# A new order for the first part of an attention and two-layer MoE kernel, and later places for the last attention pairs

## The chip, the cores and the metric

The kernel runs on one core of one Trainium2 chip. The metric is the device time of one launch in microseconds (us). The kernel before takes 853.68 us, the median of 3 runs (851.36 to 854.92).

## The reference

Three stages follow one another: an attention with two branches, a feed-forward layer with a gate (MoE 1), and one with a leaky relu (MoE 2).

```python
# attention: 4 batches, 8 heads, 576 positions, 64 features
q_d, k_d, v_d = [x.reshape(B, H, S // 4, 4, D).mean(axis=3) for x in (q, k, v)]
out_d = sm_attn(q_d, k_d, v_d)               # softmax over 144 pooled keys
out_up = np.repeat(out_d, 4, axis=2)
mask = np.abs(pos[:, None] - pos[None, :]) < 4
out_local = softmax(np.where(mask, scale * q @ k.T, -1e9)) @ v
x = out_up + out_local                       # to (2304 tokens, 512)
# MoE 1, then MoE 2, each 512 -> 2048 -> 512
h = x @ w_in;  g = h / (1 + np.exp(-1.702 * h));  x = g @ w_out
h = x @ w_in;  g = np.maximum(0.01 * h, h);       x = g @ w_out
```

The layers' weights arrive as float64 and are taken apart into a high and a low float32r part in the kernel. A product in MoE 1 is the sum of three matmuls: high by high, high by low, low by high.

## The kernel before

**Attention.** 16 jobs, one for each batch and pair of heads: job n is batch n // 4, pair n % 4. A job computes the scores in the band and those over the pooled keys, the two softmaxes, transposes the probabilities (`pt`, `pdt`, or by way of DRAM for late jobs: `td`, `pT`, `tdd`, `pdT`), multiplies with the values (`av` L684 and L700, `avd` L632 and L700) and adds the two results (`x`, L734).

**MoE 1.** 80 units: 5 blocks of tokens (512, 512, 512, 384, 384) by 16 chunks of the hidden dimension. A unit is its first layer (`l1_part`, L860: 12 matmuls into `h`), its gate (L879 on ScalarE, L880 on VectorE, a high copy L159, a low part L886) and its second layer (`l2`, L901: 12 matmuls into the four `acc` banks). The input of a block is split into `xh` (L159, ScalarE) and `xl` (L843) for each of its four feature chunks.

**Weights.** A chunk is loaded (L168), its sign and exponent taken by ScalarE (L187), its low word shifted (L188) and joined (L192) by VectorE, the high part copied (L159) and the low part subtracted (L211). The loaded words lie in one of three staging buffers, so the load of a chunk waits until the joining step of the chunk three loads earlier has read its buffer. MoE 2 follows from 491 us on and is not touched.

**What sets the order.** The kernel is under a manual schedule: each engine works through its instructions in the order in which the program issues them. The first part is a list of tokens, `ORDER` (L52 to L82): jobs 0 to 7, the weights of MoE 1, and its first 14 units, one token for each step. `w.n` loads half chunk n, `wF wL wB wH wO` are the five steps named above; `S` are the scores in the band, `E` their exponentials, `Rc` the reciprocal of the sums (L519, L520), `Mu` the division (L482), `T`/`U` the transposes and `C`/`D` the copies of them, `Va`/`Vb` the pooling of values (L440), `Kd`/`Qd` that of keys and queries (L427), `Vd` and `Y` the products with the values, `X` the sum of both branches, `xh`/`xl` the two parts of a feature chunk, `h0`/`h1` the first matmuls of units 0 and 1 by feature chunk, `L.n` the first layer of unit n, `Gt Gd Gh Gl` its gate, `M.n` its second layer. `.n` is the job, half chunk or unit. `z3.14` are 14 matmuls on a tile of zeros into bank `acc3`, whose result nobody reads (L1225). A token ends in `@V` or `@G` where it runs on VectorE or GpSimd rather than on its usual engine.

Block 0 of MoE 1 needs the first 512 tokens of all four pairs of batch 0, so `L.2`, the first unit issued in one piece, needs `xh.3` and `xl.3`, which need pair 3's `Y` products, which need its transposes, which need `Mu.3`.

From unit 14 on a loop goes over the units. After the gate of unit u come the steps listed under turn 2u, then (here, around unit 33) the second layer of the unit two before, then the steps under turn 2u+1. The later jobs 8 to 15 put their groups of steps there: group i of job n at turn `TURN + PERIOD*(n-JOBS) + i`, which is 24 + 6(n-8) + i.

Of the kernel before, what the change touches and what calls it, by code (L numbers as in the profile page):

```python
# [27 lines left out]
def attn_moe_kernel(ctx: ExitStack, tc, qT_d, kT_d, vh_d, vg_d, w1a, w2a, w1b, w2b, outT):  # L28
    nc = tc.nc
    B, NP = qT_d.shape[:2]  # L30
    DM, NT = outT.shape
# [15 lines left out]
    V, G = nc.vector, nc.gpsimd  # L47
# [5 lines left out]
        w.2 wF.2 wL.2 k.0 Kd.0 wB.2 wH.2 q.0 Qd.0 z3.14 S0.0 M0.0 S1.0 M1.0 va.4 Va0.4 Va1.4 w.0 wF.0 Sd.0 Mxd.0 Exd.0  # L53
        wO.2 wL.0 N0.0 E0.0 N1.0 Rcd.0 Mud.0 wB.0 wH.0 wO.0 k.1 q.1 z3.16 S0.1 Qd.1 Kd.1 M0.1 w.3 wF.3 wL.3 q.2 Sd.1
        Mxd.1 E1.0 Rc.0 Exd.1 vb.4 Vb0.4 wB.3 wH.3 wO.3 Vb1.4 Mu.0 Rcd.1 Mud.1 N0.1 E0.1 T0.0 C0.0 T1.0 C1.0 q.4 k.4
        z3.1 S.4 A1.4 k.2 va.1 w.1 wF.1 S1.1 M1.1 A0.4 Qd.2 Kd.2 Mx.4 Sb.4 z3.4 S0.2 M0.2 w.5 vb.7 wF.5 Qd.4 Sd.2 Mxd.2
        Exd.2 U0.0 D0.0 wL.5 N1.1 Kd.4 T0.1 k.3 z3.6 Sd.4 Rcd.2 Mud.2 wL.1 E1.1 Mxd.4 Exd.4 T1.1 C1.1 q.3 N0.2 E0.2 wB.5
        wH.5 wB.1 vb.2 Rc.1 Mu.1 Rcd.4 Mud.4 q.5 vb.0 k.5 z3.5 S.5 Qd.5 A1.5 Qd.3 A0.5 Kd.3 z3.6 U1.1 D1.1 S1.2 T0.2
        Kd.5 w.7 M1.2 wH.1 C0.1 wO.5 Vb0.7 U1.0 D1.0 wO.1 Mx.5 Sb.5 N1.2 Sd.3 S0.3 M0.3 Mxd.3 T1.4 wF.7 wL.7 va.0 T1.2
        w.4 wF.4 wL.4 w.6 wF.6 N0.3 wB.7 wB.4 E1.2 Rc.2 Mu.2 Ex.5 Exd.3 Rcd.3 Mud.3 C0.2 T0.4 C0.4 z3.4 S1.3 Vd.0 M1.3  # L60
        vh.0 Y0.0 k.6 va.6 va.5 vb.1 vh.4 C1.2 Od.0 X0.0 U0.1 D0.1 E0.3 wH.7 wO.7 C1.4 Ex.4 Y1.0 vh.1 va.2 vh.2 w.12
        vb.3 Vd.1 Od.1 w.9 X1.0 xh.0 wL.6 xl.0 N1.3 E1.3 Sm.5 wB.6 Sm.4 Rc.4 Mu.4 Rc.5 Sd.5 Mxd.5 T0.3 C0.3 Vd.4 Od.4
# [5 lines left out]
        Vb1.5 L.6 wF.15 Va0.6 wL.15 wB.19 Gt.3 wO.14@V wB.15 T0.5 T1.5 C0.5 w.10 wF.10 wL.10 wH.19 wO.19 M.0 M.1 C1.5
        Vd.5 Gd.3 Gh.3 Gl.3 wB.10 wH.10 wO.10 Va1.6 Sd.6 Mxd.6 M.2 L.4 Od.5@V va.7 w.16 Gt.6 Gd.6 wF.16 wL.16 Exd.6 w.11
        wF.11 Rcd.6 Gh.6 wL.11 wB.11 wH.11 wB.16 wH.15 Gl.6@V wO.15 S.6 A0.6 A1.6 Mx.6 Mud.6 Sb.6 wO.11@V Gt.4 Gd.4  # L70
        wH.16 wO.16@V w.22 Gh.4 Gl.4@V wF.22 wL.22 vh.5 w.13 wF.13 wL.13 vb.6 w.20 wF.20 wL.20 M.3 U1.5 D1.5 U0.5 D0.5
        wB.13 wH.13 wO.13 L.5 Gt.5 wB.20 wH.20 Gd.5 Gh.5 Gl.5 Ex.6 wB.22 wH.22 wO.22 L.7 q.7 Qd.7 k.7 Kd.7 S.7 A1.7
        wO.20 Sm.6 Gt.7 Gd.7 M.4 w.18 wF.18 wL.18 wB.18 Gh.7 Gl.7@V wH.18 wO.18 Rc.6 A0.7 Mx.7 Sb.7 w.17 wF.17 wL.17 L.8
        Gt.8 Gd.8 M.5 M.6 Y0.5 t.22 w.24 X0.5 Gh.8 Gl.8@V Vb0.6 w.26 wF.26 wL.26 wB.26 Y1.5 L.9 Gt.9 wH.26 T1.6 C1.6
        w.28 wB.17 Gd.9 Gh.9 L.10 X1.5 Sd.7 Ex.7 wO.26 Mu.6@V wH.17 Gl.9@V wO.17 M.7 M.8 Sm.7 Gt.10 Gd.10 Rc.7 wF.24
        wL.24 wF.28 wL.28 wB.24 w.21 wF.21 wL.21 Mxd.7 wB.21 wB.28 wH.24 Gh.10 Gl.10@V Vb1.6 U0.6 D0.6 Exd.7 Rcd.7 Va0.7
        wH.28 L.11 Gt.11 Gd.11 T0.6 C0.6 U1.6 D1.6 Gh.11 wO.24 Mu.7@V Mud.7 wO.28@V M.9 w.23 wF.23 wL.23 wH.21 Vd.6 Od.6
        vh.6 Y1.6 w.25 wF.25 w.27 X1.6 Va1.7 Gl.11@V wB.23 wO.21@V Vb1.7 wL.25 wB.25 wF.27 wL.27 wH.23@V wO.23 L.12
        Gt.12 Gd.12 T0.7 C0.7 T1.7 L.13 t.25 wH.25 wO.25@V C1.7 w.29 w.31 Y0.6 X0.6 U0.7 D0.7 Gh.12 wF.29 wL.29 M.10
        U1.7 D1.7 Vd.7 Od.7 wB.27 wH.27 wO.27 Gl.12@V Gt.13 wF.31 Gd.13 Gh.13 Gl.13 wB.29 vh.7 Y0.7 X0.7 w.30 wF.30 Y1.7  # L80
        X1.7 wL.31 M.11 wL.30 wB.31 wH.31 wH.29 wO.29 wB.30 wH.30 wO.30 wO.31 t.27
# [1296 lines left out]
```

## Time and profile before

| | |
|---|---|
| runs, median | 853.68 us (851.36 to 854.92) |
| profiled execution | 853.28 us, of which the span of instructions is 851.5 us |
| TensorE (PE) | 839.5 us busy, 99% of the span, 5736 matmuls |
| VectorE (DVE), ScalarE (ACT), GpSimd (POOL) | 63%, 48%, 56% busy |
| chain that ended last | PE 92%, DVE 3%, ACT 1%, DMA 1% |
| mean granted TensorE clock | 0.998 of full speed |

Matmuls are pipelined: each is shown from its start to its modelled end, so the rows overlap and the distance of two starts is what one costs. A wait in the list of waits is idle time just ahead of an instruction, put down to what came last. "SPq" rows are the issue of a DMA; the data lands later.

### The profile page before, as it was taken

What the parts mean: (1) busy time and instruction counts of PE and PEld (TensorE: products, weight loads), DVE (VectorE), ACT (ScalarE), POOL (GpSimd) and SP (SyncE); (2) the same over time, 40 slices, a digit from 0 to 9 for tenths busy, and PEclk for the clock granted to TensorE, in tenths of its full rate; (3) what the DMA queues carried; (4) which work ended last, traced back from release to release, by engine and by line L of the source; (5) the groups of instructions that cost most, each with busy time, mean ns of one, the idle gap of its engine ahead of it and who ended that gap; (6) DMA issues with size and microseconds to landing.
All of it is one profiled execution on the core that took longest, in us unless ns stands there. A gap on an engine that the chain in (4) does not pass through costs nothing.

```text
span 851.5 us, 15694 instructions
## 1 busy us (share of the span) xinstructions
PE 839.5 (99%) x5736; PEld 762.6 (90%) x5736; DVE 539.5 (63%) x950; ACT 405.5 (48%) x972; POOL 475.2 (56%) x470
## 2 busy tenths in 40 slices
...
GB/s 292 250 161 183 183 144 157 116 238 170 196 191 144 221 132 101 341 335 420 370 150 324 343 268 277 334 248 259 265 257 353 286 235 271 267 287 266 221 190 181
DMA packets 76877, 204.95 MB, mean 241 GB/s; under 512 B 14656, under 2 KB 30016, under 8 KB 70400
## 3 DMA queue, kind: packets, MB, share of 16 engines
...
HBM read 155.42 MB, written 48.50 MB: 239 GB/s over the span
## 4 chain that ended last, share of the span: by engine, by line
PE 92%; DVE 3%; ACT 1%; DMA 1%; issue 1%; SPq 1%; POOL 0%; DVEq 0%; POOLq 0%; ACTq 0%
PE h L860 23%; PE acc L901 22%; PE p L1107 21%; PE h L1032 21%; PE avd L632 1%; PE scd L549 1%; PE sc L455 1%; PE av L684 1%; DMA s<-w1a 1%; PE idle L1225 1%; ACT a L510 1%; PE av L700 0%; DMA pT<-td 0%; PE pt L651 0%; DVE s L188 0%
## 5 line engine op out<-in xcount | busy, mean ns | idle before, releaser
L1086 POOL TENSOR_TENSOR ring<-raw,ring 128x384 fp32r<-128x384 f32 x148 | 166.5, 1136 | 144.3 <-ACT ring L1084 142.8
L860 PE MATMUL h<-xh,w 128*128 128x512 f32 (+1 forms) x640 | 198.6, 373 | 0.0
L1107 PE MATMUL p<-ring,v 128*128 128x384 f32 x900 | 178.9, 334 | 0.0
L901 PE MATMUL acc<-gh,w 128*128 128x512 f32 (+1 forms) x560 | 173.2, 372 | 0.0
L1107 PEld LDWEIGHTS p<-ring,v 128*128 128x128 f32 x900 | 158.1, 188 | 0.1
L1032 PE MATMUL h<-x,v 128*128 128x384 f32 x672 | 137.4, 334 | 0.0
L860 PEld LDWEIGHTS h<-xh,w 128*128 128x128 f32 x640 | 119.1, 188 | 17.3 <-issue 1.4
L886 POOL TENSOR_TENSOR gl<-g,gh 128x512 fp32r<-128x512 f32 (+1 forms) x59 | 71.8, 1216 | 97.2 <-ACT gh L159 96.5
L1032 PEld LDWEIGHTS h<-x,v 128*128 128x128 f32 x672 | 118.4, 188 | 0.0
L860 PE MATMUL h<-xl,w 128*128 128x512 f32 (+1 forms) x320 | 117.9, 368 | 0.0
L901 PEld LDWEIGHTS acc<-gh,w 128*128 128x128 f32 x560 | 104.1, 188 | 14.8 <-issue 0.4
L901 PE MATMUL acc<-gl,w 128*128 128x512 f32 (+1 forms) x280 | 103.7, 370 | 0.0
L880 DVE SCALAR_TENSOR_TENSOR g<-g,h 128x512 f32<-128x512 f32 (+1 forms) x80 | 50.4, 630 | 79.1 <-ACT g L879 78.6
L879 ACT ACTIVATE g<-h 128x512 f32<-128x512 f32 (+1 forms) x80 | 44.0, 550 | 100.5 <-PE h L860 96.7
L1039 ACT ACTIVATE raw<-raw 128x384 f32<-128x384 f32 x72 | 37.9, 526 | 109.1 <-DVE raw L1042 108.9
L1072 DVE TENSOR_TENSOR raw<-raw,raw 128x384 f32<-128x384 f32 x84 | 76.7, 946 | 15.1 <-ACT raw L1039 13.0
L1042 DVE TENSOR_TENSOR raw<-h,u 128x384 f32<-128x384 f32 x72 | 40.1, 557 | 72.1 <-PE h L1032 71.6
L1084 ACT ACTIVATE ring<-raw 128x384 fp32r<-128x384 f32 x150 | 73.5, 515 | 0.0
L1032 PE MATMUL h<-x_ra,v 128*128 128x384 f32 x336 | 72.5, 334 | 0.0
L159 ACT ACTIVATE gh<-g 128x512 fp32r<-128x512 f32 (+1 forms) x70 | 41.7, 595 | 62.7 <-DVE g L880 58.8
L860 PEld LDWEIGHTS h<-xl,w 128*128 128x128 f32 x320 | 60.4, 189 | 6.9
L211 POOL TENSOR_TENSOR w<-t,w 128x512 fp32r<-128x512 f32 x25 | 33.1, 1327 | 48.5 <-ACT w L159 42.2
(188 smaller groups left out, 1271.3 us busy)
## 6 DMA issues: line engine op xcount, KB each, us to landing
...
v<-ws SPq DMA_DIRECT2D x72, 512.0 KB, 4.6
...
s<-w1a SPq DMA_DIRECT2D x16, 512.0 KB, 4.6
s<-w2a SPq DMA_DIRECT2D x16, 512.0 KB, 4.6
s<-w1b SPq DMA_DIRECT2D x16, 512.0 KB, 5.8
s<-w2b SPq DMA_DIRECT2D x16, 512.0 KB, 9.4
...
```

Of the source, the lines that this page charges most:

```text
L159: return nc.scalar.activation(out=out, in_=in_, func=AF.Copy, scale=scale)
L860: nc.tensor.matmul(h, w[:, kc * P : (kc + 1) * P], xs[kc][part], start=kc == 0 and i == 0, stop=kc == KC - 1 and i == 2,)
L879: lambda: nc.scalar.activation(out=g, in_=h[:, :n], func=AF.Tanh, scale=0.5 * 1.702),
L880: lambda: nc.vector.scalar_tensor_tensor(out=g, in0=g, scalar=1.0, in1=h[:, :n], op0=ALU.add, op1=ALU.mult),
L886: lambda: on(G).tensor_tensor(out=gl, in0=g, in1=gh.bitcast(F32), op=ALU.subtract),
L901: nc.tensor.matmul(acc[c][:, :n], w[:, cs], g, start=m == 0 and i == 0, stop=m == NM - 1 and i == 2)
L1032: nc.tensor.matmul(h, w[:, a, ks], x, start=not more and kt == 0 and k == 0, stop=kt == 1 and k == 2, skip_group_check=True,)
L1042: nc.vector.tensor_tensor(out=out, in0=h, in1=u, op=ALU.add)
L1072: nc.vector.tensor_tensor(out=o, in0=a, in1=b, op=ALU.subtract)
L1084: nc.scalar.activation(out=hi, in_=t, func=AF.Copy)
L1086: e.tensor_tensor(out=lo, in0=t, in1=hi.bitcast(F32), op=ALU.subtract)
L1107: nc.tensor.matmul(self.bank[pair, ct][:, :N2], w[:, q, a, cs], g, start=not more and q == 0 and k == 0, stop=q == QC - 1 and k == 2, skip ...
```

## The change

The tokens of `ORDER` are ordered anew as a whole. They are the same steps, but for the matmuls on zeros (59 where there were 56) and for the engine of some: `Va0.4`, `Va1.4`, `Va0.5`, `Mu.2`, `Mu.4`, `wO.6` and the copies `D1.2`, `D0.4` go to VectorE ahead of unit 2, `xl.1`, `Mu.5`, `wO.12` and `Kd.6` to GpSimd, for which the pooling of keys has a second form with three additions. In the loop, job 14's groups come one turn later and job 15's two; the group with the products with the values comes a further turn later for jobs 13, 14 and 15, and the last job's store sits at 15 of its slots.

```diff
-        ... xh.0 wL.6 xl.0 N1.3 E1.3 Sm.5 wB.6 Sm.4 Rc.4 Mu.4 Rc.5 Sd.5 Mxd.5 T0.3 C0.3 Vd.4 Od.4
-        wF.9 wH.4 wO.4 va.3 q.6 Vd.2 Y1.1 X1.1 h0.0 h1.0 U0.2 D0.2 T1.3 w.14 vh.3 Kd.6 Va0.5 Va1.5 Exd.5 Rc.3 C1.3 Y0.1
-        U1.2 D1.2 X0.1 Qd.6 U1.4 D1.4 wL.9 Od.2 wH.6 xh.1 Y1.2 Y0.2 X1.2 Mu.3 U1.3 D1.3 U0.3 D0.3 X0.2 wF.12 xh.2 wB.9
-        U0.4 D0.4 xl.1@V wO.6 xl.2 Y1.4 Vd.3 wH.9 wO.9 Od.3 Y0.3 X0.3 Y1.3 X1.3 xh.3 h0.1 wL.12 xl.3@V wF.14 wL.14 wB.12
-        L.2 Gt.2 Gd.2 ...
+        ... Rc.5 xh.0 Sd.5 wH.4 Sm.4 xl.0 Y1.1 q.6 Rc.4
+        wL.6 Vd.2 C0.3 X1.1 E1.3 Vd.4 w.14 Mxd.5 T1.3 wF.9 Od.4 h1.0 Exd.5 Rc.3 U1.2 wB.6 Y0.1 Od.2 Mu.4@V D1.2@V wO.4
+        X0.1 U0.2 wF.12 Va1.5 Qd.6 Mu.3 D0.2 vh.3 h0.0 U0.3 D0.3 Kd.6@G C1.3 wL.12 U1.4 Rcd.5 w.19 D1.4 wL.9 Y0.2 xh.1
+        wH.6 U1.3 X0.2 Y1.2 wB.12 X1.2 U0.4 D1.3 wH.12 xh.2 xl.1 Vd.3 wB.9 Od.3 wH.9 Y0.3 h0.1 wF.14 xl.2 wO.6@V Y1.3
+        wF.19 D0.4@V X0.3 X1.3 wL.19 xh.3 Mu.5 xl.3@V wB.19 Y1.4 L.2 ...
-    UNITS, JOBS = 14, 8
+    UNITS, JOBS, STRETCH = 14, 8, 13
         def pool4(self, dst, src):
+            if chosen[0] is G:
+                x = src.rearrange("p (g r) -> p r g", r=FACTOR)
+                G.tensor_tensor(out=dst, in0=x[:, 0], in1=x[:, 1], op=ALU.add)
+                for r in range(2, FACTOR):
+                    G.tensor_tensor(out=dst, in0=dst, in1=x[:, r], op=ALU.add)
+                return
-                14 if self is jobs[-1] else 13: "Vd Y Od X0 X1",
-                16: "O",
+                13 + (NP * self.b + self.p >= STRETCH): "Vd Y Od X0 X1",
+                15 if self is jobs[-1] else 16: "O",
-            turns.setdefault(TURN + PERIOD * (n - JOBS) + i, []).extend(fs)
+            turns.setdefault(TURN + PERIOD * (n - JOBS) + max(n - STRETCH, 0) + i, []).extend(fs)
```

GpSimd around the division of pair 3, before. `P_1_0_4` and `P_1_1_4` are the probabilities of jobs 4 and 5, `a_0_2` and `a_0_3` those of pairs 2 and 3 of batch 0.

```order
L482 TENSOR_TENSOR a_0_2_1_302<-a_0_2_1_302,stat_0_2_6_304 128x640
L530 TENSOR_TENSOR a_0_3_2_468<-a_0_3_2_468,stat_d_0_3_7_470 128x3x128
L532 TENSOR_TENSOR a_0_3_2_468<-a_0_3_2_468,stat_d_0_3_7_470 128x3x64
L211 TENSOR_TENSOR w_0_3_646<-t_0_3_1_645,w_0_3_646 128x512
L843 TENSOR_TENSOR xl_0_0_807<-xf_0_0_150,xh_0_0_806 128x512
L482 TENSOR_TENSOR P_1_0_4_215<-P_1_0_4_215,stat_1_0_7_218 128x640
L211 TENSOR_TENSOR w_0_2_439<-t_0_2_0_657,w_0_2_439 128x512
L440 TENSOR_TENSOR vg_1_1_13_744<-vg_1_1_13_744 96x2x128
L440 TENSOR_TENSOR vd_1_1_3_528<-vg_1_1_13_744 96x128
L482 TENSOR_TENSOR a_0_3_1_467<-a_0_3_1_467,stat_0_3_6_469 128x640
```

GpSimd at the same place, after (line numbers past L430 are 6 higher).

```order
L536 TENSOR_TENSOR a_0_3_2_492<-a_0_3_2_492,stat_d_0_3_7_494 128x3x128
L538 TENSOR_TENSOR a_0_3_2_492<-a_0_3_2_492,stat_d_0_3_7_494 128x3x64
L211 TENSOR_TENSOR w_0_3_627<-t_0_3_1_629,w_0_3_627 128x512
L446 TENSOR_TENSOR vg_1_3_9_187<-vg_1_3_9_187 48x2x128
L849 TENSOR_TENSOR xl_0_0_821<-xf_0_0_150,xh_0_0_820 128x512
L211 TENSOR_TENSOR w_0_2_425<-t_0_2_0_658,w_0_2_425 128x512
L446 TENSOR_TENSOR vd_1_1_3_516<-vg_1_1_13_692 96x128
L488 TENSOR_TENSOR a_0_3_1_491<-a_0_3_1_491,stat_0_3_6_493 128x640
```

The divisions of pair 2 and of job 4, and one pooling of values, no longer stand in front of that of pair 3 (`a_0_3_1`).

ScalarE ahead of `xh.3`, before and then after. `t_0_6_0` is half chunk 12, `t_0_7_0` half chunk 14, `t_0_9_1` half chunk 19.

```order
L187 ACTIVATE t_0_6_0_974<-s_0_6_0_782 128x512
L159 ACTIVATE xh_0_2_977<-xf_0_2_152 128x512
L159 ACTIVATE pT_1_0_5_216<-pt_1_0_23_981 128x384
L159 ACTIVATE w_0_4_847<-t_0_4_1_846 128x512
L159 ACTIVATE a_0_3_0_466<-avd_0_3_21_998 128x144
L159 ACTIVATE xh_0_3_1039<-xf_0_3_153 128x512
```

```order
L159 ACTIVATE w_0_6_922<-t_0_6_0_921 128x512
L159 ACTIVATE xh_0_2_993<-xf_0_2_152 128x512
L159 ACTIVATE a_0_3_0_490<-avd_0_3_21_997 128x144
L159 ACTIVATE w_0_4_882<-t_0_4_1_881 128x512
L187 ACTIVATE t_0_7_0_1027<-s_0_7_0_873 128x512
L187 ACTIVATE t_0_9_1_1041<-s_0_9_1_948 128x512
L159 ACTIVATE xh_0_3_1051<-xf_0_3_153 128x512
```

The first steps of half chunks 14 and 19 now stand ahead of `xh.3`; the staging buffer of half chunk 19 is the one that half chunk 12 had.

VectorE in the loop at units 33 and 34, before and then after. `x_3_1` is the result of job 13, `g_2_1` the gate of unit 33, `g_2_2` that of unit 34, `y` the output of block 1.

```order
L880 SCALAR_TENSOR_TENSOR g_2_1_3495<-g_2_1_3495,h_2_1_3482 128x512
L911 TENSOR_SCALAR y_1_0_3519<-acc_1_0_2305 128x512
L911 TENSOR_SCALAR y_1_2_3525<-acc_1_2_2313 128x512
L188 TENSOR_SCALAR s_1_4_0_3269<-s_1_4_0_3269 128x512
L734 TENSOR_TENSOR x_3_1_23_3564<-avd_3_1_20_3535,od_3_1_22_3561 128x288
```

```order
L886 SCALAR_TENSOR_TENSOR g_2_1_3486<-g_2_1_3486,h_2_1_3473 128x512
L917 TENSOR_SCALAR y_1_0_3519<-acc_1_0_2310 128x512
L917 TENSOR_SCALAR y_1_2_3525<-acc_1_2_2318 128x512
L188 TENSOR_SCALAR s_1_4_0_3274<-s_1_4_0_3274 128x512
L886 SCALAR_TENSOR_TENSOR g_2_2_3553<-g_2_2_3553,h_2_2_3540 128x512
L740 TENSOR_TENSOR x_3_1_23_3589<-avd_3_1_20_3560,od_3_1_22_3586 128x288
```

Job 13's result now stands behind the gate of unit 34, and on TensorE its products with the values behind the first layer of unit 34.

## Rows read from the trace of the kernel before

**Rows 1.** Windows: length, busy time by engine, clock, DMA share, GB/s

```profile
core 0: us, PE busy (x) PEld busy (x) DVE busy (x) ACT busy (x) POOL busy (x), PEclk, DMA share, GB/s
0.00:57.65 57.65, 51.70 (x705) 35.33 (x705) 44.05 (x105) 43.50 (x170) 35.13 (x47) 1.00 0.76 239
57.65:143.12 85.47, 85.47 (x649) 68.50 (x647) 62.46 (x120) 48.09 (x98) 32.14 (x30) 1.00 0.51 165
...
268.15:280.02 11.87, 9.78 (x85) 7.36 (x84) 6.36 (x15) 5.13 (x15) 4.91 (x8) 0.86 0.90 264
```

**Rows 2.** Windows of line 1225 alone, the matmuls on zeros

```profile
0.00:57.65 57.65, 15.42 (x56) 5.65 (x56) 1.00 0.76 239
```

**Rows 3.** TensorE's waits in the whole span: us in total, times, longest

```profile
PE avd L700 <- DMA pT<-td: 1.3, 1, 1.3
...
PE avd L632 <- DMA pdT<-tdd: 0.7, 1, 0.7
...
PE pt L651 <- POOL a L482: 0.4, 1, 0.4
```

**Rows 4.** Chain of waits between 200 and 290 us: start, duration, what

```profile
206.59 2.72 PE h L860 x12
209.31 2.72 PE acc L901 x12
212.03 0.71 PE avd L632 x6
...
217.13 2.72 PE acc L901 x12
...
270.74 3.32 DMA pT<-td
```

**Rows 5.** Timeline of TensorE between 268 and 283 us

```profile
271.71 1.09 PE L632 MATMUL avd<-pdT,vd 96*64 96x160 f32 x8 [0.68 <-DMA pdT<-tdd]
274.11 0.27 PE L700 MATMUL avd<-pT,vh 64*64 64x64 f32 x1 [1.31 <-DMA pT<-td]
```

**Rows 6.** Timeline of GpSimd between 42 and 62 us

```profile
50.88 1.25 POOL L482 TENSOR_TENSOR a<-a,stat 128x640 f32<-128x640 f32 x1
52.09 1.26 POOL L211 TENSOR_TENSOR w<-t,w 128x512 fp32r<-128x512 f32 x1
```

**Rows 7.** Timeline of ScalarE between 42 and 62 us

```profile
45.15 0.23 ACT L510 ACTIVATION_READ_ACCUMULATOR a<-sc,stat 128x1 f32 x1
45.24 0.51 ACT L159 ACTIVATE a<-pdt 128x384 f32<-128x384 f32 x1
...
47.08 0.68 ACT L187 ACTIVATE t<-s 128x512 f32<-128x512 f32 x1 [1.17 <-DMA s<-w2a]
47.67 0.61 ACT L159 ACTIVATE w<-t 128x512 fp32r<-128x512 f32 x1
```

**Rows 8.** Timeline of VectorE between 42 and 62 us

```profile
48.02 0.17 DVE L519 TENSOR_SCALAR stat<-stat 128x10 f32<-128x10 f32 x1
...
52.29 1.61 DVE L192 SCALAR_TENSOR_TENSOR t<-t,s 128x512 uint32<-128x512 uint32 x1
...
58.04 0.69 DVE L843 TENSOR_TENSOR xl<-xf,xh 128x512 fp32r<-128x512 f32 x1 [0.23 <-ACT xh L159]
...
58.98 0.68 DVE L192 SCALAR_TENSOR_TENSOR t<-t,s 128x512 uint32<-128x512 uint32 x1
```

**Rows 9.** Timeline of TensorE between 40 and 62 us

```profile
50.43 1.38 PE L684 MATMUL av<-a,a 64*64 64x58 f32 x40
52.19 0.77 PE L651 MATMUL pt<-ident,a 128*128 128x128 f32 x5 [0.38 <-POOL a L482]
...
59.95 0.39 PE L860 MATMUL h<-xl,w 128*128 128x512 f32 x1
```

**Rows 10.** The page's DMA issues: count, KB each, us to landing

```profile
s<-w2a SPq DMA_DIRECT2D x16, 512.0 KB, 4.6
...
xf<-xd SPq DMA_DIRECT2D x4, 192.0 KB, 11.5
```

More of the change, by code (lines that the diff above doesn't have):

```diff
@@ L52, in attn_moe_kernel @@
     ORDER = """
[L53 to L62, printed above, removed]
@@ L63, in attn_moe_kernel @@
-        wF.9 wH.4 wO.4 va.3 q.6 Vd.2 Y1.1 X1.1 h0.0 h1.0 U0.2 D0.2 T1.3 w.14 vh.3 Kd.6 Va0.5 Va1.5 Exd.5 Rc.3 C1.3 Y0.1
-        U1.2 D1.2 X0.1 Qd.6 U1.4 D1.4 wL.9 Od.2 wH.6 xh.1 Y1.2 Y0.2 X1.2 Mu.3 U1.3 D1.3 U0.3 D0.3 X0.2 wF.12 xh.2 wB.9
-        U0.4 D0.4 xl.1@V wO.6 xl.2 Y1.4 Vd.3 wH.9 wO.9 Od.3 Y0.3 X0.3 Y1.3 X1.3 xh.3 h0.1 wL.12 xl.3@V wF.14 wL.14 wB.12
-        L.2 Gt.2 Gd.2 wH.12 wO.12@V Gh.2 Gl.2@V vb.5 Vb0.5 Rcd.5 Mud.5 w.8 wF.8 wL.8 h1.1 h1.2 h1.3 Gt.1 Gd.1 Gh.1 wB.14
-        wB.8 wH.8 Gl.1@V Mu.5@V L.3 wO.8 h0.2 h0.3 Y0.4 Gt.0 Gd.0 Gh.0 X0.4 w.19 wF.19 w.15 wH.14 X1.4 Gl.0@V wL.19
@@ L68, in attn_moe_kernel @@
[L68 to L81, printed above, removed]
+        w.0 k.0 wF.0 va.4 q.0 wL.0 w.3 vb.7 wB.0 wF.3 wH.0 k.2 wO.0 z3.15 q.1 S1.0 S0.0 w.2 Va0.4@V Qd.0 wL.3 Kd.0 Sd.0
```

25 lines of the change are left out of this document (added).

## The prediction, made before the changed kernel ran

> **What bounds the kernel now.** I read the windows first. From 57.65 us, where the first layer of unit 2 starts, TensorE is busy for all of the 85.47 us to the end of the first part; its share of busy time in the 57.65 us before is lower, and 15.42 us of that are the matmuls on zeros, which nobody waits for [rows 1, 2]. So the first part's order can move the end of the kernel in one way only: by when unit 2 runs through. What stands behind it is the same work without a gap, as long as the new order opens none.
>
> Then the list of waits. In the whole span it names three waits that matter here: 0.4 us behind a division on GpSimd, and, on the transfers of late jobs, 0.7 and 1.3 us, each once [rows 3]. The timeline puts these last two at 271.0 and 272.8 us, at job 13's products with the values [rows 5], and in the window from 268.15 to 280.02 us the mean granted clock is 0.86 where it is 1.00 in the two windows above it [rows 1]. So there are two places to look at: the stall of job 13, which lies on the path in full because TensorE has nothing else queued, and the chain to unit 2.
>
> **The stall of job 13.** Away from it the chain shows the same cycle undisturbed: second layer at 209.31, products of a late job at 212.03, and the next second layer at 217.13, so 7.82 us from one to the next [rows 4]. At job 13 the same stretch takes 11.87 us [rows 1]. The difference is 4.05 us: 0.68 + 1.31 = 1.99 us of waits [rows 5], and 2.06 us of slower matmuls. The clock explains most of the second part: 14% of 11.87 us is 1.66 us, which is what 3.3 us at 1.2 GHz instead of 2.4 GHz give.
>
> What the change does there: the products come behind the first layer of unit 34, 2.72 us of matmuls by an undisturbed row [rows 4], which depend on nothing of job 13 and whose bank was free long before (unit 32's gate). The load of pT, issued at 270.74, lands at 274.06 [rows 4]; SP's instructions ahead of it are the same, since only groups behind it move. TensorE ends the second layer at 268.15 + 2.72 = 270.87, the first layer of unit 34 at 273.59 and the first six products, which need only pdT (there at 271.71, rows 5), at about 274.30. That is 0.24 us after pT. So both waits go and with them the cause of the low clock. I take 4.05 us. The bounds: if 0.3 us of wait remain and the clock stays, 3.7; nothing can be won beyond 4.05, since without waits the stretch is the undisturbed one.
>
> The result of job 13 then stands on VectorE behind unit 34's gate and leaves a bank of the pair `h` later. Two first layers lie between, over 5 us, so unit 36 finds it free: nothing. Jobs 14 and 15 had no wait before; each of their groups keeps the distance to its own load or gains one or two turns (2.72 us each, rows 4). The last store moves one turn later, about two units ahead of the loads that read it: nothing. If such a load came late, it would show as a wait at the start of block 3, and cost what it waits.
>
> **The first part: which chain, before.** The last wait ahead of unit 2 is at 52.19, for the division of pair 3 on GpSimd (50.88, 1.25 us) [rows 6, 9]. Its exponentials were done on ScalarE at 45.38 [rows 7]. In between lie 6.8 us for a reciprocal, at 48.02 [rows 8], and this division, together 1.7 us of work. The other 5.1 us are queues: on GpSimd the divisions of pair 2 and of job 4 and two poolings of values, and the low part of half chunk 4, whose high part ScalarE copies only at 47.67, behind a load that landed at 47.08 [rows 7].
>
> **After.** I count what stands ahead of each link in its queue. On ScalarE up to the end of pair 3's exponentials: two more copies, of half chunk 4 and of a pdt tile; by their rows with the overlap of neighbours taken off, 0.5 us each [rows 7], 0.95 in all. On VectorE up to the reciprocal: two instructions fewer, four more, +0.9 us at the engine's mean of 44.05 / 105 = 0.42 us [rows 1], against 13.6 us in which it idles before 57.65. On GpSimd up to the division: five fewer and none more; half chunk 4's copy now comes ahead of the exponentials, so the division follows its reciprocal at once. The loads start in another order: pair 1's keys are the twelfth load instead of the sixth, with some 1,450 KB more ahead, 6.2 us at 239 GB/s [rows 1]. ScalarE idles 14.15 us in this stretch and takes most of that back; I bound what is left at pair 3's exponentials by 0 and 2.3 us and take 1.0, nearer to the first. So these end at 45.38 + 0.95 + 1.0 = 47.3 (46.3 to 48.6), the reciprocal at 47.7, the division at 49.1.
>
> From there two chains lead to unit 2's last low product, at 59.95 before [rows 9].
> - TensorE: from the transposes at 52.19 to unit 2's start there were 5.46 us. Behind them now come the transposes and products of pair 2 as well: 40 small matmuls, 1.38 us, and four transposes at 0.15 us [rows 9], 2.0 us. 49.1 + 5.46 + 2.0 = 56.6 for the start, 58.9 for that product: 1.05 us earlier than before. Three more matmuls on zeros lie where TensorE idles.
> - The new link: half chunk 19 is taken apart on ScalarE ahead of `xh.3` and on VectorE ahead of `xl.3`. Its load waits until half chunk 12 is joined on VectorE; twelve instructions after the reciprocal at 0.42 us are 5.0 us, so 52.7. It lands 4.6 us later [rows 10], 57.3, then follow the first step (0.6), `xh.3` (0.55, as the copy in rows 7) and `xl.3` (0.69, rows 8): 59.1, 0.85 us earlier than 59.95.
>
> Both give about the same, 0.9 us. Against that stands what VectorE and GpSimd take from each other. At 52.29 a joining step took 1.61 us beside GpSimd's L211 of 52.09, and 0.68 at 58.98 with GpSimd free [rows 6, 8]: 0.93 us lost. In the new order a joining step (half chunk 6), then a division of 640 elements moved to VectorE, stand right behind the reciprocal, where GpSimd runs pair 3's division. One such loss on the second chain would leave nothing of the gain. I take half of it: a gain of 0.5 us, with bounds of +1.9 (exponentials at 46.3, no loss) and -1.4 (48.6, with the loss).
>
> The Trainium skill's page "SBUF — State Buffer" (section "SBUF: two separate sides") says that VectorE with two inputs in SBUF and GpSimd take their common pair of ports as a lock for a whole instruction, and the other waits. The rows of 52.09 and 52.29 agree with it. By that rule the loss comes in full here, and the first part would give about 0; that result is among the rivals below.
>
> **Sum.** The profiled execution took 853.28 us, 1.78 of it outside the span. 853.28 - 4.05 - 0.5 = 848.7; it lies 0.4 below the median of the runs, so I forecast 849.1 us as a median (849.0 rounded), 0.55% less.
>
> **Rivals.**
> 1. The first part saves more: ScalarE takes all of its lag back, no joins collide, and unit 2 comes 1.5 to 1.9 us earlier, in the extreme by the 4.2 us that are queue and not work (5.1 less 0.9). 853.7 - 4.05 - 1.7 = 847.9, at most 845.4. For it: five instructions fewer ahead of the division. Against it: VectorE gets ten more instructions up to `xl.3`, about 4 us at 0.42.
> 2. The first part gives nothing or costs: GpSimd and VectorE collide, by the rule above, or the load of half chunk 19 holds `xl.3`. 849.6 at 0, 851.0 at -1.4.
> 3. The stall only moves, so that the change does not do what it says: pT lands later than 0.24 us past its time before, since other transfers (0.90 of the engines busy, rows 1) meet it. A landing 2 us later brings the wait back and with it the low clock, and about 0.4 us of 4.05 stay won: 852.8. Against it: the same issues ahead of it at the same time.
> 4. Slower: the one link that is new and serial, half chunk 19. All of ScalarE stands behind its first step. The longest landing on the page for a transfer of less size is 11.5 us [rows 10]; then 52.7 + 11.5 + 1.85 = 66.1 for `xl.3`, 6.1 us past 59.95, and TensorE idles before it, so that up to 3.3 us at 1.2 GHz add 1.65: 853.7 - 4.05 + 7.8 = 857.5. It decides against the forecast's sign from a landing at 62.2 (59.95 + 4.05 - 1.85). Against it: loads of its kind took 4.6 us in the median [rows 10].
>
> **How the numbers follow.** Forecast 0.60 (its own range 847.6 to 849.9); rival 1 0.17; rival 2 0.12; rival 3 0.07; rival 4 0.04. The measurement of this kernel can't tell less than about 0.5%, 4.27 us, from no change, so the border is 849.4. Of the forecast 0.38 lies below it, with rival 1 0.55; the rest of the forecast, rivals 2 and 3 are the same, 0.41; rival 4 is slower, 0.04. The range goes from the extreme of rival 1 past the end of rival 2, and leaves out rivals 3 and 4: 845.4 to 852.0.
>
> **What would show it.** No wait of `avd` and `av` for pdT or pT around 274 us, and a clock of 1.00 there, so that the stretch takes 7.8 plus the 2.72 of unit 34 between; a wait left would be rival 3. The first layer of unit 2 starting near 57 us, with the division of pair 3 right behind its reciprocal near 48: a start before 56 would be rival 1, past 57.7 rival 2. ScalarE idle for half chunk 19's load just ahead of `xh.3` is the new link at work. And no gap on TensorE between unit 2 and 143 us: one would be a wait that I have not seen, and the forecast wrong by its length.

## The result: slower by 1.3%, and the profile after

The changed kernel takes 864.08 us in the median (863.18 to 867.91), the kernel before 853.43 us beside it: a ratio of 1.0131, 95% interval 1.0101 to 1.0161. Forecast were 849.0 us. One run of e6 (2,935 us) and one of e11 (924 us) were slowed as a whole and are left out of the medians and ratios below. The profiled execution has a span of 862.8 us, 11.3 us more than before.

The windows of the changed kernel, with the columns of [rows 1]; the last one is the stretch in which job 13 stalled before:

```profile
0.00:57.65 57.65, 48.55 (x560) 31.65 (x562) 43.97 (x97) 37.85 (x157) 29.70 (x42) 0.91 0.76 238
57.65:143.12 85.47, 81.87 (x643) 64.31 (x642) 67.21 (x113) 45.41 (x92) 43.48 (x34) 1.00 0.44 143
...
268.15:280.02 11.87, 11.44 (x90) 8.76 (x86) 9.80 (x19) 5.16 (x15) 8.62 (x8) 1.00 0.31 89
```

The granted clock, 1.00 in the first window before, is 0.91; the second window, in which TensorE was busy throughout, has 3.6 us of gaps. TensorE's waits in the whole span (the columns of [rows 3]):

```profile
PE avd L638 <- DMA a<-vg: 3.6, 1, 3.6
PE sc L455 <- ACT a L516: 3.6, 1, 3.6
PE h L866 <- DVE xf L740: 1.6, 1, 1.6
PE pdt L585 <- DVE P L475: 1.1, 1, 1.1
PE h L866 <- POOL xl L849: 1.0, 2, 0.6
...
PE acc L907 <- DVE gl L892: 0.7, 1, 0.7
```

The waits of job 13 [rows 3] are gone. In their place stand six others, five of them in the first part. To add them up I take four starts on ScalarE from the traces: A, the first of pair 3's last five exponentials (`E1.3`, which end 1.6 us later); B, the gate of unit 2, which follows its first layer; C, the gate of unit 17; and the distance from the gate of unit 30 to that of unit 36, around job 13. In us:

| kernel | A | A to B | B to C | 30 to 36 | ratio of times, 95% |
|---|---|---|---|---|---|
| before | 43.80 | 16.80 | 104.04 | 43.38 | 1 |
| changed | 47.53 | 23.51 | 108.54 | 40.09 | 1.0101 to 1.0161 |
| e1_late_only | 44.09 | 16.09 | 104.03 | 40.07 | 0.9962 to 0.9987 |
| e2_order_only | 45.47 | 23.16 | 108.41 | 43.39 | 1.0115 to 1.0160 |
| e3_va2_early | 49.66 | 19.77 | 108.07 | 40.10 | 1.0103 to 1.0145 |
| e4_warm | 49.51 | 20.38 | 107.84 | 40.06 | 1.0096 to 1.0148 |
| e5_engines | 49.69 | 18.22 | 107.80 | 40.05 | 1.0098 to 1.0143 |
| e6_shift_late | 49.98 | 21.21 | 108.69 | 40.05 | 1.0111 to 1.0149 |
| e7_chain | 49.07 | 20.54 | 108.30 | 40.05 | 1.0081 to 1.0116 |
| e8_late13 | 44.38 | 16.94 | 104.04 | 39.71 | 0.9957 to 0.9980 |
| e9_own_x | 49.90 | 19.08 | 108.10 | 40.07 | 1.0079 to 1.0129 |
| e10_links | 49.88 | 17.31 | 108.20 | 40.07 | 1.0068 to 1.0115 |
| e11_loads | 46.65 | 18.91 | 107.84 | 40.07 | 1.0043 to 1.0095 |
| e12_mu3 | 43.32 | 16.38 | 104.04 | 39.71 | 0.9950 to 0.9976 |
| e13_old_engines | 46.27 | 16.82 | 108.15 | 40.07 | 1.0057 to 1.0106 |
| e14_tail | 46.22 | 17.19 | 108.38 | 40.07 | 1.0039 to 1.0079 |
| e15_va2_late | 42.90 | 23.14 | 104.04 | 41.85 | 1.0048 to 1.0085 |

Changed against before: +3.73 up to A, +6.71 from A to B, +4.50 from B to C, -3.29 around job 13; the sum, 11.65, is the span's 11.3 but for 0.35 elsewhere. One row is one execution: two kernels with the same first part (changed and e2; e11 and e14) differ by 2.1 and 0.4 us at A, and e11 and e14 by 1.7 from A to B, so a difference of 2 us in the first two columns is not shown by one row alone. From B to C the kernels with the new order lie within 0.9 us of each other, those with the old one within 0.01. Around job 13 kernels with the same places lie within 0.05 us, but for e15: its places are those of before, its clock stayed at 1.00 there, and it takes 41.85 instead of 43.38.

Much of what differs at A goes with TensorE's clock. Windows of e2, then of e3 (the columns of [rows 1]):

```profile
0.00:40.00 40.00, 35.41 (x421) 21.40 (x421) 32.05 (x73) 28.22 (x118) 21.30 (x33) 1.00 0.84 264
0.00:40.00 40.00, 35.35 (x370) 21.62 (x371) 28.62 (x64) 24.09 (x101) 21.08 (x32) 0.87 0.79 251
```

Ahead of A the traces show no time at 1.2 GHz in e2, e11, e13, e14 and all kernels with the old order, 3.4 us in the changed kernel, e5 and e6, 6.8 us in e4 and e7, and 10.2 us in e3, e9 and e10. In the changed kernel the clock fell at 23.49, right behind the wait of 3.6 us for ScalarE (L455 above). With the new order A is at 45.5 to 46.7 where the clock did not fall and at 47.5 to 50.0 where it did. So rows are best compared where this time is the same, as in e3, e9 and e10.

**Where A to B went.** SP's issues in the changed kernel (start, duration; the rows of line 380 and 381 are the values of pair 3, then of pair 2):

```profile
36.84 1.82 SPq L385 DMA_DIRECT2D a<-vg  x4
38.71 1.56 SPq L401 DMA_DIRECT2D a<-vh  x1
40.32 1.83 SPq L385 DMA_DIRECT2D a<-vg  x4
42.19 0.42 SPq L401 DMA_DIRECT2D vh<-vh  x1
42.71 0.38 SPq L168 DMA_DIRECT2D s<-w1a  x1
43.13 0.43 SPq L380 DMA_DIRECT2D a<-vg  x1
43.60 0.43 SPq L381 DMA_DIRECT2D a<-vg  x1
44.07 0.42 SPq L380 DMA_DIRECT2D a<-vg  x1
44.54 0.42 SPq L381 DMA_DIRECT2D a<-vg  x1
```

Before, pair 2's values were issued at 37.04, ahead of half chunk 12 and of the last values of pair 3; now at 44.07, behind the thirteen issues shown. The chain of waits shows what that does (start, duration, what), and TensorE's timeline the wait and the matmuls behind it:

```profile
44.54 5.91 DMA a<-vg
50.58 4.05 PE avd L638 x28
...
55.41 1.28 PE h L866 x3
```

```profile
46.31 0.67 PE L690 MATMUL av<-a,a 64*64 64x58 f32 x16
50.58 2.70 PE L638 MATMUL avd<-a,a 128*64 128x144 f32 x20 [3.60 <-DMA a<-vg]
53.21 1.42 PE L638 MATMUL avd<-pdT,vd 96*64 96x144 f32 x8
54.56 0.85 PE L585 MATMUL pdt<-ident,a 128*64 128x128 f32 x3
55.06 0.78 PE L866 MATMUL h<-xh,w 128*128 128x512 f32 x1
```

The 20 matmuls take 2.70 us where 20 of the same form took 1.59 at 43.02: behind its wait of 3.6 us TensorE was given 1.2 GHz (0.66 is the mean granted clock from 50 to 60 us). The next row, the products of job 4 (`Vd.4`), ends at 54.63, and GpSimd's timeline goes on from there:

```profile
54.78 0.45 POOL L446 TENSOR_TENSOR vd<-vg 96x128 f32<-96x128 f32 x1 [5.48 <-DVE P L488]
55.19 1.26 POOL L488 TENSOR_TENSOR a<-a,stat 128x640 f32<-128x640 f32 x1
```

The first row is `Va1.5`, the second `Mu.3`, pair 3's division. `Va1.5` overwrites pooled values that `Vd.4` reads, so it waits for TensorE (the profile names VectorE's Mu.4, which ended just before; in e3 and e4 below it starts 0.1 to 0.2 us after `Vd.4`, whatever Mu.4 does). So one load holds `Vd.2`, `Vd.4`, `Va1.5`, `Mu.3` and with it all of pair 3; `Mu.3` starts 2.2 us after its reciprocal, which ended at 52.96. VectorE's rows show a second wait, in front of this reciprocal, which begins with the row at 52.54:

```profile
49.51 0.32 DVE L740 TENSOR_TENSOR xf<-av,a 128x164 f32<-128x164 f32 x1
51.69 0.22 DVE L740 TENSOR_TENSOR x<-av,a 128x64 f32<-128x64 f32 x1 [1.86 <-DMA xd<-x]
51.83 0.60 DVE L562 TENSOR_REDUCE scd<-scd 128x3 f32<-128x432 f32 x1
52.47 0.16 DVE L566 TENSOR_SCALAR stat_d<-scd 128x3 f32<-128x3 f32 x1
52.54 0.16 DVE L525 TENSOR_SCALAR stat<-stat 128x10 f32<-128x10 f32 x1
```

X1.1 writes the one shared tile from which the store of X1.0 still reads. Before, that wait was shorter, and it stood ahead of the reciprocal too, which came at 48.02 [rows 8]:

```profile
47.21 0.22 DVE L734 TENSOR_TENSOR x<-av,a 128x64 f32<-128x64 f32 x1 [0.49 <-DMA xd<-x]
```

A third wait is ScalarE's, just ahead of `xh.3`:

```profile
67.11 1.24 ACT L187 ACTIVATE t<-s 128x512 f32<-128x512 f32 x2 [2.48 <-DVE w L211]
```

These are the first steps of half chunks 14 and 19. What the profile shows to end their wait is `wO.6`, which the change moved to VectorE and which ended at 67.04: it reads one of the three buffers `t` that these steps write. The load of half chunk 19 had landed at 65.89.

**Around job 13.** The chain of the changed kernel shows job 13's products between first layer and second layer without a wait. TensorE's timeline shows a new wait some fourteen microseconds earlier, at the start of block 2:

```profile
286.74 2.72 PE h L866 x12
289.46 0.64 PE avd L638 x5
...
291.61 2.95 PE acc L907 x12
```

```profile
273.97 0.39 PE L866 MATMUL h<-xh,w 128*128 128x512 f32 x1
...
275.47 0.50 PE L866 MATMUL h<-xl,w 128*128 128x512 f32 x1 [0.43 <-POOL xl L849]
```

Job 14's scores, 0.74 us, no longer stand ahead of unit 32's first layer, so that this now waits 0.43 us for GpSimd's low parts.

### The profile page after: what moved, and what is told of

It is laid out like the page before. It is cut to its first block, busy times and chain, and to the rows that moved or that the text cites. A ratio compares the mean times of both kernels' runs of the same rounds, so it can differ in the third digit from the quotient of the medians.

```text
span 862.8 us, 15685 instructions
## 1 busy us (share of the span) xinstructions
PE 845.5 (98%) x5739; PEld 763.9 (89%) x5739; DVE 556.3 (64%) x956; ACT 404.1 (47%) x968; POOL 483.1 (56%) x470
## 4 chain that ended last, share of the span: by engine, by line
PE 86%; DVE 6%; DMA 2%; ACT 2%; issue 1%; POOL 1%; SPq 1%; DVEq 0%; ACTq 0%; POOLq 0%
PE acc L907 21%; PE p L1113 20%; PE h L1038 20%; PE h L866 20%; PE avd L638 1%; DVE t L192 1%; DMA s<-w2a 1%; PE scd L555 1%; DVE s L188 1%; PE sc L461 1%; DMA a<-vg 1%; POOL xl L849 1%; DMA vg<-vg 1%; PE av L690 1%; DVE w L211 1%
## 5 line engine op out<-in xcount | busy, mean ns | idle before, releaser
L892 POOL TENSOR_TENSOR gl<-g,gh 128x512 fp32r<-128x512 f32 (+1 forms) x62 | 77.5, 1250 | 98.4 <-ACT gh L159 98.4
L907 PEld LDWEIGHTS acc<-gl,w 128*128 128x128 f32 x280 | 52.6, 188 | 7.9 <-DVE gl L892 1.1
## 6 DMA issues: line engine op xcount, KB each, us to landing
ws<-wo SPq DMA_DIRECT2D x16, 1792.0 KB, 10.2
```

Source lines behind the costliest of these rows:

```text
L892: lambda: on(G).tensor_tensor(out=gl, in0=g, in1=gh.bitcast(F32), op=ALU.subtract),
L907: nc.tensor.matmul(acc[c][:, :n], w[:, cs], g, start=m == 0 and i == 0, stop=m == NM - 1 and i == 2)
```

## The experiments

**Late places alone, and the order alone.** e1 has the new `slots` and `turns` with the old `ORDER`, e2 the new `ORDER` (and the second form of `pool4`) with the old places.

> The kernel before with the new places of the late groups alone. Theory A (the loss is all in the first part, the late places win): job 13's stretch loses its 4.2 us, the first layer at the start of block 2 pays up to 0.7 for its low parts; 849.5 to 850.3 against 853.4, waits of avd for pT and pdT gone. Rival B (the late places cost as well): 853 or more.

> The changed kernel with the late groups where they were. Theory A: unit 2 ends 10.4 us later than before, unit 14 starts 14.0 later, unit 16 loses 0.9 more, and job 13's stall is back: 853.4 + 14.9 = 868 (867 to 869). Rival B: less than the 864.1 of the changed kernel.

e1: 850.4 us, ratio 0.9974 (0.9962 to 0.9987), 0.1 us above the range expected; the stretch around job 13 is 40.07 us and all else as before. e2: 864.64, 3.4 us less than expected: its stretch around job 13 is 43.39 as it should, but its profiled execution, in which the clock did not fall ahead of A, came to A 2.1 us earlier than that of the changed kernel. On the sign both theories A hold: the late places win 0.26%, all of the loss is the order's. That the late places win as much inside the changed kernel is not shown by its time, which is 0.6 us below that of e2, with overlapping intervals.

**The load of pair 2's values.**

```diff
-        ... vb.1 / vh.1 Sb.5 ... C1.4 va.2 w.9 ...
+        ... vb.1 / va.2 vh.1 Sb.5 ... C1.4 w.9 ...
```

> The changed kernel with one load, the values of pair 2, issued ahead of vh.1 instead of eight loads later. Theory A (that load holds Vd.2, and behind it Vd.4, Va1.5 and the division of pair 3): the wait of 3.6 us goes, TensorE stays at full clock from 50 to 57 us, Mu.3 follows Rc.3 at once; unit 2 ends 3 to 7 us earlier than in the changed kernel, 857 to 861. Rival C (VectorE's longer queue sets unit 2's time, the load only fills an idle wait): unit 2 moves by less than 1 us, 863 to 864.

The wait of `avd` is gone from the list, the 20 matmuls take 1.59 us, and `Mu.3` follows its reciprocal. GpSimd's rows in e3:

```profile
51.56 0.48 POOL L446 TENSOR_TENSOR vd<-vg 96x128 f32<-96x128 f32 x1
53.99 1.52 POOL L488 TENSOR_TENSOR a<-a,stat 128x640 f32<-128x640 f32 x1 [1.94 <-DVE stat L526]
```

From A to B e3 takes 19.77 us, 3.7 less than the changed kernel. But the time is 863.36, which its interval does not tell from 864.08, since A came 2.1 us later in it and the chain then met the next waits (2.5 us for `X0.3`). The low clock that followed the load's wait is gone, but the clock fell ahead of A instead. The theory holds for the mechanism, the rival for the size: that the load costs the changed kernel time is not shown.

**The clock behind that wait.** 16 matmuls on zeros ahead of `Vd.2`:

```diff
-        wL.6 Vd.2 C0.3
+        wL.6 z0.16 Vd.2 C0.3
```

> The changed kernel with 16 more matmuls on zeros (3.5 us by the rows of the others) ahead of Vd.2, which waits 3.6 us there. Tells what the low clock behind that wait costs by itself: if it sits on the path, Vd.2, Vd.4 and h1.0 run in 2.8 us instead of 5.4 and unit 2 ends 2 to 2.6 us earlier, 861.5 to 862.2. Rival C (VectorE's queue sets the time): the matmuls are faster and unit 2 ends where it did, 864.

```profile
48.88 3.63 PE L1231 MATMUL idle<-warm 128*128 128x512 bf16 x16
52.44 1.59 PE L638 MATMUL avd<-a,a 128*64 128x144 f32 x20
53.96 0.86 PE L638 MATMUL avd<-pdT,vd 96*64 96x144 f32 x8
```

`Vd.2` to `h1.0` run in 3.4 us instead of 5.9, A to B is 3.1 us shorter, and the time 862.62 (1.0096 to 1.0148), 0.4 above the range expected and again not told from 864.08. e3 and e4 shorten A to B by about the same. But A came 2 us later in both, so how much of the late load's price is the wait and how much the clock behind it is not shown.

**The engines.** e5 puts each of the 38 tokens whose engine differs, 11 of them ahead of unit 2, back on the engine that it had before.

```diff
-        ... Va0.4@V ... Mu.2@V ... Mu.4@V D1.2@V ... Kd.6@G ... wO.6@V ... D0.4@V ...
+        ... Va0.4 ... Mu.2 ... Mu.4 D1.2 ... Kd.6 ... wO.6 ... D0.4 ...
```

> The changed kernel's order with every step on the engine that it had before (38 tokens lose or gain their suffix). Theory D (the order, by what each in-order queue waits for, makes the loss): va.2 still holds Vd.2, and Mu.3 stands behind Va1.5 again; 862 to 866. Rival C (the sharing, that is VectorE's ten more instructions and their collisions with GpSimd): at least half of the loss goes, 858 or less.

862.35: the order makes the loss, not the sharing. `Va1.5` waits for `Vd.4`, which the profile names here, and the load of va.2 holds `Vd.2` for 1.9 us. In this execution the clock did not fall behind that wait.

**Links one after the other.** e6 and e7 build on e3, e9 on e3, e10 on e9, e11 on e10.

```diff
 # e6
-        z3.1 wL.2 z3.5 ... Mud.1 wB.2
+        z3.1 z3.5 ... Mud.1 wL.2 wB.2
 # e7
-        C0.3 X1.1 E1.3 Vd.4 ... Exd.5 Rc.3 U1.2 ... xl.2 wO.6@V Y1.3 wF.19 D0.4@V X0.3 X1.3 wL.19
+        C0.3 E1.3 Rc.3 X1.1 Vd.4 ... Exd.5 U1.2 ... xl.2 Y1.3 wF.19 X0.3 X1.3 wO.6@V D0.4@V wL.19
 # e9
-    SLOT_TAGS = (("q", "kT", "qd", "kd", "od"), ...
+    SLOT_TAGS = (("q", "kT", "qd", "kd", "od", "x"), ...
-            if not self.first or tag in ("stat", "stat_d", "x"):
+            if not self.first or tag in ("stat", "stat_d"):
-                    x = self.tile([P, S], "x")[:, :w]
+                    x = self.tile([P, w if self.first else S], "x")[:, :w]
 # e10
-        wF.14 xl.2 wO.6@V Y1.3 wF.19 D0.4@V X0.3 X1.3 wL.19 xh.3 Mu.5 xl.3@V wB.19 Y1.4 L.2
+        xl.2 Y1.3 X0.3 X1.3 xh.3 D0.4@V xl.3@V wO.6@V wF.14 wF.19 wL.19 Mu.5 wB.19 Y1.4 L.2
 # e11
-        w.0 k.0 wF.0 va.4 q.0 wL.0 w.3 vb.7 ... k.2 wO.0 z3.15 q.1 ... Va0.4@V Qd.0 ... va.1 M0.0 k.1
+        w.0 k.0 wF.0 q.0 wL.0 w.3 k.1 q.1 ... va.4 wO.0 z3.15 k.2 ... Qd.0 ... vb.7 va.1 M0.0 Va0.4@V
```

> e3_va2_early with the shift wL.2 behind the divisors of pairs 0 and 1 on VectorE instead of ahead of pair 1's maxima, where it took 2.6 us in the changed kernel beside GpSimd's Mud.0 and wO.3. Theory E (an early collision delays pair 1 by 2 us and the delay is carried to unit 2): E0.1 and all that follows, pair 3's exponentials too, 2 us earlier, 860.5 to 861.8. Rival: the early lag is absorbed by idle matmuls and the later queue, 863 as e3.

> e3_va2_early with two more edits of VectorE's order: the reciprocal of pair 3 ahead of X1.1, which waits for the store of X1.0 to have read its tile, and X0.3, X1.3 ahead of wO.6 and D0.4. Theory D (what stands ahead in VectorE's queue waits or collides): Rc.3 follows E1.3 within 1 us (2.3 to 3.9 before this edit), xh.3 no longer waits for X0.3 behind wO.6; unit 2 3 to 5 us earlier than in e3, 858.5 to 860.5. Rival (VectorE's sum of work, whatever its order): less than 1 us, 862.5 to 863.5.

> e3_va2_early with a place of its own for the rest of each first pair's result, in the job's slot instead of the one shared tile, so that X1.1, X1.2 and X1.3 wait for no store. Theory D (in-order queues behind a wait): Rc.3 follows E1.3 within 2 us (2.7 in e3) and X1.2, X1.3 no longer stop VectorE; unit 2 1 to 2.5 us earlier, 861 to 862.5. Rival: VectorE has other work to do in that time and unit 2 stays, 863.4.

> e9_own_x with VectorE's and ScalarE's last steps ahead of unit 2 in the order of need: X0.3 and X1.3 ahead of wO.6 and D0.4, and the first steps of half chunks 14 and 19 behind xh.3 and xl.3. Theory D: nothing that waits for half chunk 19 or collides stands ahead of xh.3 any more; from Rc.3 to the end of xl.3 12 us instead of 14 to 17 (10.3 before the change), 858.5 to 860.5. Rival (total work of VectorE): 861 or more.

> e10_links with the first loads in the old spirit: keys and queries of pair 1 fifth and sixth, va.4, vb.7 and k.2 behind them, and Va0.4 behind M0.0. Theory F (the start lag comes from pair 1's late keys): Kd.1 ends 1 to 2 us earlier, and all of pair 1 to 3 with it; E1.3 ends at 47 to 49 instead of 50 to 51, 857 to 858.5. Rival G (VectorE is busy 93 to 95% from 20 to 50 us and sets E1.3 whenever pair 1 starts): E1.3 within 0.7 us of e10, the same time.

e6, 863.29: a miss. The shift takes 0.39 us instead of 1.9 and pair 1's exponentials come 1.5 us earlier, but A is where it was in e3. The lag has another cause, in which the clock (1.2 GHz for 3.4 us from 32.86) may have a part. e7, 861.16, 0.7 above the range expected: `Mu.3` comes 2.1 us earlier than in e3 and B does not, since ScalarE then waits ahead of `xh.3` with the first step of half chunk 19 (its row, then `xh.3`):

```profile
66.87 0.66 ACT L187 ACTIVATE t<-s 128x512 f32<-128x512 f32 x1 [2.43 <-DVE w L211]
67.44 0.61 ACT L159 ACTIVATE xh<-xf 128x512 fp32r<-128x512 f32 x1
```

X1.3 had been done at 65.7. This is the step that rival 4 of the prediction named, but not its price: the load had landed at 64.82. The step waits for `wO.6` on VectorE, which ran from 65.60 to 66.84 and which this edit had put behind X1.3. The clock also fell at 55.28 in this execution.

e3, e9 and e10 have the same 10.2 us at 1.2 GHz ahead of A, none behind it, and A within 0.3 us, so their rows compare well. e9, 861.8: X1.1, X1.2 and X1.3 wait for no store, and A to B is 0.7 us shorter. e10, 860.22: with these last steps in the order of need A to B is 17.31, 1.8 less again.

e11, 858.68, 0.2 above the range expected: A comes 3.2 us earlier than in e10, as theory F said. That pair 1's keys alone make this is not shown. The clock did not fall ahead of A in e11, as it did for 10.2 us in e10; and e2, with the keys as late as in the changed kernel and no fall of the clock either, has A at 45.47, before e11's 46.65. What is shown is that in the three traces with this start (e11, e13 and e14) the clock does not fall ahead of A, and that A is at 46.2 to 46.7 there.

No two neighbours of this row of kernels are told apart by their intervals; the changed kernel and e11 are (1.0131 and 1.0069).

**What is left.** e13 is e11 with the old engines ahead of unit 2 (11 tokens), e14 is e11 with two edits behind it:

```diff
-        wL.16 w.15 C1.5 Gl.0@V ... t.22 T1.6 Gl.5@V wF.17 wF.26 M.5 Y0.5 Gd.7 wO.18@V M.6
+        Gl.0@V wL.16 w.15 C1.5 ... t.22 Gl.5@V wF.17 wF.26 M.5 Y0.5 Gd.7 wO.18@V M.6 T1.6
```

> e11_loads with the steps ahead of unit 2 on the engines that they had before (11 tokens). Theory C (sharing: Mu.4, Va0.5, wO.6 and others on VectorE make its queue longer and collide): of the 5.0 us that unit 2 is still late at least 2.5 go, 856 to 857. Theory D (order): unit 2 within 1 us of e11, 859 to 860; what is left is which product stands behind which division on TensorE.

> e11_loads with two edits behind unit 2: the low part of unit 0's gate ahead of the shift of half chunk 16, which waits for its load, and the transposes T1.6 behind M.6, since their bank is freed by A1.7, late in VectorE's queue. Expected if these two waits (0.7 and 1.1 us in the changed kernel) are on the path: both gone from TensorE's list, unit 14 1.8 us earlier, 857.6. Rival: the next wait comes in their place, 859 to 859.5.

e13, 859.22, is not told from e11, and e14, whose first part is e11's, has the same A to B as e13 within 0.4 us: once more no difference by the engines is shown. In these two rows, with the links mended and the clock at 1.00, A to B is what it was before (16.8 to 17.2); in e11 itself, where the clock fell at 52.81, it is 18.9. e14, 857.9, is near the 857.6 expected, but its interval does not part it from e11, and from B to C it is no shorter (108.38). The wait for the transposes is gone, but one for a load of values of 1.1 us has come, and unit 0's low part is waited for 1.1 instead of 0.7 us. The 4 us from B to C are not one wait but several, and not waits alone: in the changed kernel TensorE starts the same 773 matmuls between B and C as before, is idle for 2.6 us, and busy for 105.96 instead of 104.04 us at a clock of 1.00. Why the same matmuls take 1.9 us longer in the new order, and which order removes the waits, stays open.

**The load, put into the kernel before.**

```diff
-        vh.1 va.2 vh.2 ... va.3 q.6 Vd.2
+        vh.1 vh.2 ... va.3 q.6 va.2 Vd.2
```

> The kernel before with one edit: the load of pair 2's values eleven issues later, just ahead of Vd.2. Theory A: it lands near 50 us, Vd.2 waits some 6 us (43.8 before), TensorE goes to 1.2 GHz behind that wait, GpSimd's Va1.5 and Mu.3 do not hang on it here because Vd.4 stands ahead of Vd.2; unit 2 5 to 8 us later, 858 to 861. Rival: the matmuls behind it find their place in the waits that follow, unit 2 less than 3 us later, 856 or less.

```profile
47.68 2.62 PE L632 MATMUL avd<-a,a 128*64 128x144 f32 x18 [4.73 <-DMA a<-vg]
...
51.31 0.80 PE L860 MATMUL h<-xh,w 128*128 128x512 f32 x1
```

859.03, ratio 1.0067 (1.0048 to 1.0085): this one load, issued at 44.18 instead of 37.04, costs the kernel before 6 us, with a wait of 4.7 us (some 6 expected) and the low clock behind it. So it is enough by itself for about half of what the order loses (12 us in e2).

**A version that beats both.** e8 is the kernel before with job 13's group alone one turn later; e12 is e8 with the division of pair 3 ahead of what stood before it on GpSimd:

```diff
 # e8
-                14 if self is jobs[-1] else 13: "Vd Y Od X0 X1",
+                14 if self is jobs[-1] or (self.b, self.p) == (3, 1) else 13: "Vd Y Od X0 X1",
 # e12, besides
-        wH.4 wO.4 va.3 ... Va0.5 Va1.5 Exd.5 Rc.3 C1.3 ... X1.2 Mu.3 U1.3
+        wH.4 va.3 ... Exd.5 Rc.3 Mu.3 wO.4 Va0.5 Va1.5 C1.3 ... X1.2 U1.3
```

> The kernel before with one edit: the group Vd Y Od X0 X1 of job 13 one turn later, jobs 14 and 15 as before. Theory A: job 13's 4.2 us are won as in e1_late_only, and the scores of job 14 stay between the last second layer of unit 31 and the first layer of unit 32, so that the 0.7 us of waiting for low parts there are not paid; 849.3, or 0.7 less than e1_late_only. Rival: the late groups of jobs 14 and 15 were worth something in e1_late_only too; 850 to 851.

> e8_late13 with one more edit: on GpSimd the division of pair 3 stands ahead of wO.4, Va0.5 and Va1.5, right behind its reciprocal. By the prediction's reading (5.1 us of queue between exponentials and division are the reserve of the first part): U0.3 up to 2.4 us earlier and unit 2 1.5 to 2 us earlier, 848.4. By what TensorE's own waits of before say (only 0.4 and 0.6 us of idle lie there, the rest was work): unit 2 0 to 0.9 us earlier, 849.4 to 850.3.

e8: 850.28 (0.9957 to 0.9980); the stretch around job 13 is 39.71, 0.36 less than in e1 instead of the 0.7 expected, and the time is in the rival's range and not told from e1's. e12: 849.41 us, ratio 0.9963 (0.9950 to 0.9976), the lowest median here; its interval overlaps those of e1 and e8. `Mu.3` starts at 48.15, 2.7 us earlier [rows 6], but the transposes behind it only 0.9 us earlier [rows 9]:

```profile
49.47 0.41 PE L651 MATMUL pt<-ident,P 128*128 128x128 f32 x2 [0.69 <-POOL a L482]
49.99 1.38 PE L684 MATMUL av<-a,a 64*64 64x58 f32 x40
51.30 0.77 PE L651 MATMUL pt<-ident,a 128*128 128x128 f32 x5
```

B is 0.9 us earlier than before, 0.5 of it there at A already. That fits the reading by TensorE's waits, not that by the 5.1 us of queue.

## Why the prediction was wrong

**What failed: the chain to unit 2, above all "the division follows its reciprocal at once".** The first part was to gain 0.5 us (between +1.9 and -1.4); unit 2's gate came 10.4 us later. I counted what stands ahead of the division on GpSimd and found five instructions fewer, which is right, and did not ask what the ones that stayed wait for. `Va1.5` waits for `Vd.4`, that stands on TensorE behind `Vd.2`, and that waits for a load that SP issues 7 us later. The division started at 55.19 instead of 47.8. Of these 7.4 us, 2.2 are that wait behind the reciprocal; 3.4 are between the exponentials and the reciprocal, which "at 47.7" had right behind them, with the wait of X1.1 in it; and 1.8 are late exponentials. TensorE meanwhile stood for 3.6 us at the same load and then ran at 1.2 GHz. e3 takes the load away and the division follows its reciprocal, though no time is won that can be told from noise; e15 puts the load into the kernel before and loses 6 us. The prediction looked at the new place of one load (pair 1's keys) and of one half chunk, though each load in SP's list had moved.

**The price of such a wait.** Rival 4 priced a late load with the low clock behind it at 857.5, for half chunk 19, and gave it 0.04. The kind of failure was right, the load was another: half chunk 19's landed in 3.9 us. Its first step did hold ScalarE for 2.5 us ahead of `xh.3`, but for a buffer that `wO.6` on VectorE still read.

**The start.** "ScalarE takes most of that back": pair 3's exponentials ended at 49.11, where I had 47.3 and an upper bound of 48.6. In e2, with the same first part and no low clock ahead of A, they ended at 47.05, so the term as such is not shown to be wrong; what it left out is the clock, which fell ahead of A in eight of the twelve traces with the new order and in none of the five with the old one. VectorE is busy for 9.3 to 9.5 us in each 10 us from 20 to 50 us, so it had little idle time in which to catch up.

**The wait X1.1.** It stood in the trace of before (0.49 us, a store of a shared tile), and I left it out, because it was small; here it takes 1.86 us ahead of the reciprocal.

**The reserve.** "The other 5.1 us are queues" is true of the chain and was not a gain to be had: TensorE had other work in that time and waited 0.4 us. Rival 1 rested on it. e12 takes three instructions out of that queue, and in its row unit 2 comes 0.9 us earlier, 0.4 of it from A to B.

**"No gap on TensorE between unit 2 and 143 us."** From unit 2's first layer to unit 14's it takes 89.2 us instead of 85.5, and unit 16 loses 0.9 more. The prediction named such gaps as what would make it wrong by their length; I had looked for them by margins of single queues.

**VectorE's collisions.** Half a loss was taken, and the rival gave 1.4 us for them. They are there (below), but in e5 and e13 putting all steps back on their engines does not bring the time back.

**Right: job 13.** The second layer in unit 33, job 13's products and the first layer of unit 34 take 7.68 us instead of 11.87, 4.19 less, where I had 4.05, and the clock stays at 1.00. What was not seen is some 0.9 us elsewhere between units 30 and 36, with the wait at the start of block 2; the net is 3.3. Of this 1.5 us are the clock, which does not fall in every execution: in e15 the same stall took 41.85 us without it. By the times the late places win 2.1 us (e1).
